# Batch 0's start refilled and batch 1's order changed in a fused cross-attention and GELU feed-forward kernel

## Chip, cores, metric

One core of a Trainium2 chip. The metric is the device time of one execution in microseconds (us), median over executions. Every execution used here also has a span (first to last instruction); in all of them the metric is the span plus 1.75 to 1.8 us, so the two can be compared by subtracting 1.77.

## The reference

For each of 8 batches and 8 heads, x (512 x 64) and a state (32 x 64) attend to one another: a softmax of x on state, and one of state on x. The 544 rows that come out per batch are then sent through a feed-forward layer.

```python
scores = scale * np.matmul(x, state.transpose(0, 1, 3, 2))
a = softmax(scores);  xread = np.matmul(a, state)
scores2 = scale * np.matmul(state, x.transpose(0, 1, 3, 2))
a2 = softmax(scores2); sread = np.matmul(a2, x)
x = concat([xread, sread])            # per batch (512+32) x (8*64)
h = x @ w_in                          # 512 -> 2048
g = 0.5 * h * (1.0 + erf(h / sqrt(2)))
return g @ w_out                      # 2048 -> 512
```

## The kernel before

The engines are PE (TensorE, products; PEld is its weight load), ACT (ScalarE), DVE (VectorE) and POOL (GpSimd). It never forms xread. It multiplies the state by w_in first (`P`, four quarters of 512 columns per batch), so that h is `P` times the transposed softmax `AT`. The order of instructions is written by hand; each engine takes its own in that order. `M(m)` is one tile of h (`hp` in the views) and its gelu (`g`), `U(u)` four products of an output tile (`op`), four tiles of g deep. Results of products land in PSUM, TensorE's result memory, and are copied from there by ACT or DVE. ACT does exps, gelus and some copies, DVE the rest.

```python
def keep_warm(n):                     # idle products, result unused
    ps = ps_o.tile([128, 512], FP32, name="warm_ps", tag="op")
    for _ in range(n):
        nc.tensor.matmul(ps[:, 0:128], lhsT=warm, rhs=warm, start=True, stop=True)

def norm(b, half):                    # row sums, reciprocal, product: all on DVE
    nc.vector.reduce_sum(out=cs, in_=e4, axis=AX.X)
    nc.vector.reciprocal(out=ics, in_=cs)
    nc.vector.tensor_tensor(out=..., in0=e4, in1=..., op=ALU.mult)

def pmat(b, fs, act=()):              # P = state x w_in, two halves t = 0, 1
    ...                               # 8 products into two PSUM tiles
    for t in range(2):
        if t in act: nc.scalar.copy(out=dst, in_=ps[t])
        else:        nc.vector.tensor_copy(out=dst, in_=ps[t])

begin(0)
keep_warm(30)
...                                   # batch 0: scores, softmax, transposes
M(0, 1, 2, 3)
U(0, 1)
pmat(0, (1,), act=(1,))
U(2)
M(4)
U(3)
state_prep(1, B)                      # state transposes of batches 1 to 7
M(5)
begin(1)
xtr(1, (0, 1))                        # x of batch 1 transposed
xtr(1, (2, 3))
sread(0)
M(6, 7)
scores(1, 0)
scores(1, 1)
srt(0)
U(4, 5)
pmat(0, (2,))                         # third quarter of P, BEFORE norm
rearr_ones(1)
norm(1, 0)
norm(1, 1)
U(6, 7)
M(8, 9)                               # first use of the third quarter
...
```

The softmax here doesn't subtract the row's maximum and nothing guards it: scores larger than these inputs give would overflow.

## Time and profile before

| | before |
|---|---|
| median of 4 | 219.09 us (218.79 to 219.24) |
| the execution whose profile is quoted in the prediction | 220.56 us, span 218.8 |
| TensorE busy | 213.5 us, 98% |

The profile's execution is 1.4 us longer than the median beside it. That gap turns out to matter. The lines on which the argument rests are in the prediction.

### The profile page before, as it was taken

What the parts mean: (1) busy time and instruction counts of PE and PEld (TensorE: products, weight loads), DVE (VectorE), ACT (ScalarE), POOL (GpSimd) and SP (SyncE); (2) the same over time, 40 slices, a digit from 0 to 9 for tenths busy, and PEclk for the clock granted to TensorE, in tenths of its full rate; (3) what the DMA queues carried; (4) which work ended last, traced back from release to release, by engine and by line L of the source; (5) the groups of instructions that cost most, each with busy time, mean ns of one, the idle gap of its engine ahead of it and who ended that gap; (6) DMA issues with size and microseconds to landing.
All of it is one profiled execution on the core that took longest, in us unless ns stands there. A gap on an engine that the chain in (4) does not pass through costs nothing.

```text
span 218.8 us, 3962 instructions
## 1 busy us (share of the span) xinstructions
PE 213.5 (98%) x1650; PEld 102.0 (47%) x1650; DVE 84.3 (39%) x165; ACT 121.9 (56%) x216; POOL 42.4 (19%) x56
## 2 busy tenths in 40 slices
PE   7999999999999999999999999999999999999993
PEld 6644534344444445444544444444444465565442
DVE  4722593626219230942176025902381204200151
ACT  3663765579494537953774479355944463564000
POOL 7662106700133011600170016000000000000000
PEclk9999999999999999999999999999999999999998
DMA  6999999960665818282725445370042002200035
GB/s 184 183 188 204 206 202 128 217 158 0 59 89 189 116 34 99 101 199 39 96 97 155 87 52 137 116 129 0 29 171 44 3 0 99 99 0 0 12 85 194
DMA packets 38708, 22.98 MB, mean 105 GB/s; under 512 B 21921, under 2 KB 34465, under 8 KB 38689
## 3 DMA queue, kind: packets, MB, share of 16 engines
q0 software_dynamic: 13648, 8.23, 27.2%
q1 hardware_dynamic: 24352, 14.09, 25.5%
q10 hardware_dynamic: 688, 0.39, 0.6%
q8 instruction: 13, 0.21, 0.4%
q14 instruction: 7, 0.05, 0.1%
HBM read 17.30 MB, written 8.91 MB: 120 GB/s over the span
## 4 chain that ended last, share of the span: by engine, by line
PE 97%; DVE 1%; ACT 1%; issue 0%
PE op L444 50%; PE hp L395 26%; PE p_ps L356 4%; PE hps L457 3%; PE ops L469 3%; PE warm_ps L127 2%; PE opl L422 2%; PE pt L263 2%; PE sr L319 1%; PE xT_ps L206 1%; PE pc L225 1%; ACT g L402 1%; PE p_ps L378 0%; PE aT_ps L299 0%; DVE xT L211 0%; PE st_ps L136 0%
## 5 line engine op out<-in xcount | busy, mean ns | idle before, releaser
L444 PE MATMUL op<-w_out_bf,g 128*128 128x512 bf16 x496 | 118.7, 379 | 0.1
L402 ACT ACTIVATE g<-hp 128x512 bf16<-128x512 f32 x128 | 67.9, 599 | 47.0 <-PE hp L395 46.9
L444 PEld LDWEIGHTS <-g 128*128 128x128 bf16 x496 | 47.0, 98 | 59.7 <-issue 6.6
L395 PE MATMUL hp<-AT,P 128*128 128x512 bf16 x256 | 66.1, 387 | 0.1
L395 PEld LDWEIGHTS <-P 128*128 128x128 bf16 x256 | 23.7, 99 | 27.4 <-issue 2.1
L408 DVE COPY osb<-op 128x512 f32<-128x512 f32 x31 | 20.9, 687 | 33.8 <-PE op L444 33.8
L370 DVE CAST P<-p_ps 128x512 bf16<-128x512 f32 x32 | 20.9, 686 | 31.3 <-PE p_ps L356 31.2
L368 ACT CAST P<-p_ps 128x512 bf16<-128x512 f32 x30 | 16.4, 588 | 23.1 <-PE p_ps L356 19.8
L170 POOL COPY x<-xb 128x1024 bf16<-128x1024 bf16 x12 | 12.1, 1041 | 31.1 <-DMA xb<-in_x_dram 26.1
L286 DVE TENSOR_TENSOR a<-e,ics 128x512 bf16<-128x512 bf16 x14 | 12.5, 892 | 0.5
L181 POOL COPY xo<-xb 128x1024 bf16<-128x1024 bf16 x12 | 12.2, 1050 | 0.0
L615 POOL COPY hold<-P 128x1 bf16<-128x1 bf16 x4 | 0.8, 190 | 53.8 <-DVE P L370 53.8
L283 DVE TENSOR_REDUCE cs<-e 128x16 f32<-128x512 bf16 x14 | 9.5, 676 | 2.5 <-ACT e L270 2.5
L356 PE MATMUL p_ps<-w_in_bf,sbd 64*32 64x512 bf16 x248 | 10.4, 382 | 0.0
L329 DVE RECIPROCAL inv<-sr 128x2 f32<-128x2 f32 x8 | 1.3, 168 | 22.8 <-PE sr L319 22.8
L270 ACT ACT_TABLE_LOAD x7 | 9.0, 1283 | 2.0 <-issue 1.3
L402 ACT ACT_TABLE_LOAD x7 | 9.0, 1283 | 0.1
L433 ACT COPY osb<-opl 128x128 f32<-128x128 f32 x1 | 0.3, 266 | 15.2 <-PE opl L422 15.2
L408 DVE COPY osb<-ops 128x512 f32<-128x512 f32 x2 | 1.4, 692 | 18.2 <-PE ops L469 18.2
L457 PE MATMUL hps<-XSR,w_in_bf 128*128 128x256 bf16 x64 | 8.3, 272 | 0.0
L270 ACT ACTIVATE e<-pt 128x512 bf16<-128x512 f32 x14 | 7.6, 594 | 0.1
L457 PEld LDWEIGHTS <-w_in_bf 128*128 128x128 bf16 x64 | 6.3, 98 | 2.4
(66 smaller groups left out, 112.5 us busy)
## 6 DMA issues: line engine op xcount, KB each, us to landing
out_dram<-osb SPq DMA_DIRECT2D x31, 256.0 KB, 2.3
xb<-in_x_dram POOLq DMA_DIRECT2D x7, 512.0 KB, 5.8
w_in_bf<-in_moe_w_in_dram POOLq DMA_DIRECT2D x8, 256.0 KB, 10.4
w_out_bf<-in_moe_w_out_dram POOLq DMA_DIRECT2D x4, 512.0 KB, 12.8
x0f<-in_x_dram SPq DMA_DIRECT2D x2, 256.0 KB, 3.4
out_dram<-osb SPq DMA_DIRECT2D x8, 64.0 KB, 1.7
x0f<-in_x_dram ACTq DMA_DIRECT2D x1, 256.0 KB, 4.2
st_bf<-in_state_dram POOLq DMA_DIRECT2D x1, 224.0 KB, 10.3
```

The source lines that it names most:

```text
L170: nc.gpsimd.tensor_copy(out=A.x4[:, :, :, 64 * t:64 * t + 64].rearrange("p j c d -> p c j d"), in_=src[:, t],)
L181: eng.tensor_copy(out=A.xo[:, :, c0:, 2 + 64 * t:66 + 64 * t].rearrange("p j c d -> p c j d"), in_=src[:, t, c0:],)
L270: nc.scalar.activation(out=A.e[:, :, 64 * half:64 * half + 64], in_=pt.rearrange("p j t c n -> p (j t) (c n)"), func=AF.Exp, scale=scale,)
L286: nc.vector.tensor_tensor(out=A.a[:, :, hs].rearrange("p g (c n) -> p g c n", n=NS), in0=e4, in1=ics[:, :, :].to_broadcast((128, G, 2, NS) ...
L356: nc.tensor.matmul(ps[t][32 * c:32 * c + 32, :], lhsT=sbd[64 * t:64 * t + 64, b, c, 32 * t:32 * t + 32], rhs=w_in_bf[64 * t:64 * t + 64, c ...
L368: nc.scalar.copy(out=dst, in_=ps[t])
L370: nc.vector.tensor_copy(out=dst, in_=ps[t])
L395: nc.tensor.matmul(hp, lhsT=Ps[b][:, t, m * 128:(m + 1) * 128], rhs=atts[b].AT[:, :, t, :], start=(t == 0), stop=(t == 1),)
L402: nc.scalar.activation(out=gs[b][:, m, :], in_=hp, func=AF.Gelu)
L408: nc.vector.tensor_copy(out=osb, in_=ps)
L444: nc.tensor.matmul(ps, lhsT=gs[b][:, m, j * 128:(j + 1) * 128], rhs=w_out_bf[:, m, :], start=(m == 0), stop=(m == MC - 1),)
L457: nc.tensor.matmul(hp, lhsT=w_in_bf[:, c, m * 128:(m + 1) * 128], rhs=XSR[:, c, :], start=(c == 0), stop=(c == HC - 1),)
```

## The change

Its intent: keep TensorE busy from the start so that its clock rises early, shorten batch 0's chain, and reorder loads and products to suit an earlier start. The diff is cut: unchanged lines between those shown are left out.

```diff
+    load_st(1, 2)            # states of batch 1 only, ahead of x of batch 1
-    (states of batches 1 to 7 in one load here)
         for f in range(2, FC):
             load_w_in(f); load_w_out(f)
+        load_st(2, B)
         load_x(2)
-        if b == 0 and cs[0] == 3:          # which xT copy of batch 0 ACT takes
+        if b == 0 and cs[0] == 2:
-                nc.scalar.copy(out=A.AT[:, :, t, :], in_=ps)
+                nc.vector.tensor_copy(out=A.AT[:, 0:2, t, :], in_=ps[:, 0:2, :])
+                nc.scalar.copy(out=A.AT[:, 2:4, t, :], in_=ps[:, 2:4, :])
-    keep_warm(30)
+    keep_warm(32)
     xtr(0, (0,))
+    keep_warm(6)
     xtr(0, (2,))
+    keep_warm(3)
-    sums0(2)
-    sums0(3)
+    sums0(2, 3)              # one instruction
     load_rest()
+    nc.scalar.activation(out=gate, in_=gate, func=AF.Gelu)   # moved up
+    keep_warm(2)
     p0 = pmat00(0)
...
     M(0, 1, 2, 3)
-    U(0, 1)
+    U(0, 1, 2)
     pmat(0, (1,), act=(1,))
-    U(2)
-    M(4)
     U(3)
-    state_prep(1, B)
-    M(5)
+    M(4, 5)
+    state_prep(1, 2)         # 2 to 7 later, after U(12)
+    M(6)
     begin(1)
...
-    M(6, 7)
+    M(7)
     scores(1, 0)
     scores(1, 1)
     srt(0)
     U(4, 5)
-    pmat(0, (2,))
     rearr_ones(1)
     norm(1, 0)
     norm(1, 1)
-    U(6, 7)
+    U(6)
+    pmat(0, (2,), act=(1,))
+    U(7)
     M(8, 9)
```

More of the change, by code (lines that the diff above doesn't have):

```diff
@@ L104, in load_x, with load_st @@
         xbs[b] = xb
+    def load_st(b0, b1):
+        nc.gpsimd.dma_start(
+            out=st_bf[:, b0:b1, :, :].rearrange("q b t d -> q (b t) d"),
+            in_=st_rows[:, b0:b1, :, :].rearrange("q b t d -> q (b t) d"),
+        )
     load_w_in(0)
@@ L108 @@
     load_w_in(1)
-    nc.gpsimd.dma_start(
-        out=st_bf[:, 1:B, :, :].rearrange("q b t d -> q (b t) d"),
-        in_=st_rows[:, 1:B, :, :].rearrange("q b t d -> q (b t) d"),
-    )
+    load_st(1, 2)
     def load_rest():
@@ L233, in scores0, with sums0 @@
         )
-    def sums0(c):
+    def sums0(*cs):
         A = atts[0]
-        if c % 2 == 0:
+        if cs[0] % 2 == 0:
             A.sums = att.tile([128, SJ * 2, 2], FP32, name="cs", tag="cs")
+        c0, n = cs[0], len(cs)
         nc.vector.reduce_sum(
-            out=A.sums[:, :, c % 2], in_=A.e[:, :, NS * c:NS * c + NS], axis=AX.X
+            out=A.sums[:, :, c0 % 2:c0 % 2 + n],
+            in_=A.e[:, :, NS * c0:NS * (c0 + n)].rearrange("p g (c n) -> p g c n", n=NS),
+            axis=AX.X,
         )
@@ L508 @@
     scores0(3)
-    sums0(2)
-    sums0(3)
+    sums0(2, 3)
     norm0(1)
     load_rest()
+    nc.scalar.activation(out=gate, in_=gate, func=AF.Gelu)
+    keep_warm(2)
     p0 = pmat00(0)
     nc.scalar.copy(out=Ps[0][:, 0, 0:512], in_=p0)
-    nc.scalar.activation(out=gate, in_=gate, func=AF.Gelu)
     keep_warm(10)
@@ L564 @@
     U(12)
+    state_prep(2, B)
     M(16)
```

## The prediction

> **What bounds the kernel now.** I read the page first (busy time and the chain that ended last), then the chain in order of time, then the timeline of the first 40 us.
>
> ```profile
> PE 213.5 (98%) x1650; PEld 102.0 (47%) x1650; DVE 84.3 (39%) x165; ACT 121.9 (56%) x216; POOL 42.4 (19%) x56
> PE 97%; DVE 1%; ACT 1%; issue 0%
> ```
>
> TensorE is busy 98% of the span and makes 97% of the chain that ended last. A change that leaves TensorE's real work alone, as this one does, can gain only where TensorE waits, runs idle products, or runs slowly. The list of waits has no TensorE wait worth naming after about 31 us; all of it lies at the start. The timeline there:
>
> ```profile
> 0.99 3.38 PE L127 MATMUL warm_ps<-warm 128*128 128x128 bf16 x30 [0.99 <-DVE warm L75]
> 5.71 0.39 PE L225 MATMUL pc<-sbd,xT 128*128 128x64 bf16 x4 [0.58 <-DVE xT L211]
> 8.54 0.39 ACT L228 ACTIVATE e<-pc 128x256 bf16<-128x256 f32 x1
> 9.55 0.42 DVE L239 TENSOR_REDUCE cs<-e 128x8 f32<-128x256 bf16 x1 [0.16 <-ACT e L228]
> 10.29 0.69 DVE L250 TENSOR_TENSOR a<-e,ics 128x512 bf16<-128x512 bf16 x1
> 11.48 1.06 PE L299 MATMUL aT_ps<-ident,a 128*128 128x128 bf16 x8
> 12.58 0.59 ACT L301 COPY AT<-aT_ps 128x512 bf16<-128x512 bf16 x1 [0.79 <-PE aT_ps L299]
> 12.63 3.71 PE L395 MATMUL hp<-AT,P 128*128 128x512 bf16 x8
> 16.16 2.13 PE L444 MATMUL op<-w_out_bf,g 128*128 128x512 bf16 x8
> 17.03 0.76 PEld L444 LDWEIGHTS <-g 128*128 128x128 bf16 x5 [0.53 <-ACT g L402]
> ...
> 43.27 2.32 PE L395 MATMUL hp<-AT,P 128*128 128x512 bf16 x10
> ```
>
> The columns are start, duration, engine, line. The line of most use is the eight hp products at 12.63: they take 3.71 us, while ten of the same at 43.27 take 2.32. With the last one's own 0.6 and 0.38 us taken off, the step from one to the next is (3.71-0.62)/7 = 0.44 us against (2.32-0.38)/9 = 0.216. TensorE runs at **half rate** until about 16.2 us. The thirty idle products (3.38 us, 0.107 each) and the transposes run at that half rate too; in the individual starts every 128-column product before 16.2 steps by 0.107, and the same after it by 0.056. The row PEclk of the page shows 9 in these slices and hides this: the trace's clock record has its first entry only at 16.2 us. So the idle products of the kernel before do not do their job: there are holes (0.25 us before the state transpose at 4.42, 0.58 before 5.71, 0.3 before 7.05, some 0.1 each at every change of tile), and the first stretch of over 3.4 us without a hole is the one from 12.63 on.
>
> **What the Trainium skill says.** (1) "TensorE: Matmul & The Clock Gate", Part 1, The HAM clock gate: the array starts at half clock, and goes to full after one busy window of about 3.4 us; the window runs free, so the moment varies by run. This trace agrees: half steps, and the change 3.57 us after the start of the first unbroken stretch. How large a hole still counts as busy the page does not say; here about 19% of holes in the 3.4 us before 12.8 was too much. (2) The same page, Part 4, PE-mode transpose: transposes don't count as busy in the same way. If so here, the transposes of batch 0 are holes too; no view of before settles it. (3) "ScalarE: Activation LUTs", What ACT_TABLE_LOAD costs: about 1283 ns; the trace has 1.28 us at 10.29. (4) "DMA: Bandwidth & Descriptors", Why small descriptors are slow: short pieces carry a fixed overhead. In the trace the 224 KB of states take from 14.64 to 16.12, 1.48 us, of which 1.27 (6/7) is for batches 2 to 7.
>
> **The change part by part.**
>
> Idle products: 30 to 32 adds 2x0.107 = 0.21 us, ending at 4.38 instead of 4.17, just before the state transpose that waits for ACT until 4.37, so it costs nothing and closes the 0.25 us hole. Six new ones (0.64) run from 4.92 to 5.56 in the hole before 5.71: free. Three (0.32) fill 6.75 to 7.07, where TensorE waits for DVE until 7.05: free within 0.03. Two more lie in front of the first P product. So TensorE is unbroken from 1.0 to about 7.3 but for some 0.15 us: 6.3 us, nearly two windows. I expect full clock at **about 4.6 to 6.0 us** instead of 16.2.
>
> Copies of batch 0: the third xT copy goes from DVE (0.42) to ACT (0.59), the fourth from ACT to DVE. The last two row sums (2 x 0.42) become one instruction of the 128x512 form, 0.68 in the groups. At half clock this alone moves little: the single sum must wait for the last exp, so 9.3+0.68 = 10.0 where now 9.55+0.42 = 9.97. At full clock the whole chain shortens: second xT ready at 6.80, scores and the two middle exps by 8.07, fourth xT 8.00, last exp 8.32 to 8.70, DVE sum to 9.42, reciprocal 0.25 to 9.69, product 0.69 to **10.40** (before 10.98).
>
> Transposes of a: before, TensorE reaches them only at 11.48, after ten idle products at half rate and the second P product at 10.75. At full rate these are over by 10.2 (its weights land at 9.62), so they start at 10.44; four take 0.45, DVE copies 0.43 to 11.31, the second half is copied by ACT (about 0.38, as the 128x256 copies) and DVE together to about 11.6. First hp product at 11.36 (before 12.63), second at 11.63 (before 13.22).
>
> hp, gelu, first output products: ACT then sets the pace. Four gelus in a row take 2.06 us (timeline at 59.32). First hp done at 12.0, so the fourth g at 14.1 and the fourth product of the first output tile at 14.15. Before, it waited for ACT till 17.04. That is **2.9 us earlier**. The table load and the gate's gelu move ahead of the P copy, which then ends at 10.8, still before 11.36: free.
>
> Transfers: w_in's second quarter (landed 14.64) and w_out's first (12.41) are in time for TensorE at 16.4 and 12.2. With 2.9 us gained x of batch 1 (landed 18.90) would be wanted at 18.9 and w_out's second quarter (21.88) at about 21.7, so both would just bind; moving the states of 2 to 7 behind the weights brings each at least 1.27 us forward. The later quarters have over 2 us in hand. x of batch 2 has the same bytes ahead of it (34.58), and its scores come at 47.6 while its xT landed at 42.05: 5.5 us in hand. The extra seven state transposes only move (0.39 us in all).
>
> Order of products: U(2) before the P products and M(6) earlier leave less work beside the batch 1 chain of xT copies (2 x 0.645), scores, softmax of the state read (0.16+0.29) and its transpose: I count 0.2 to 0.3 us of new waits near 20 us. The gelu wait at 31 us (about 0.6 lost on the output tile) stays, as the table load sits there still.
>
> Sum: -2.9 + 0.3 = **-2.6 us**, from 219.2 to **216.6**; after 31 us TensorE is full, so the gain is kept to the end.
>
> **The rivals.**
>
> A, the clock does not come early: transposes or the 0.1 us holes break the window. For: 1.7 of 4.9 us between 4.4 and 9.3 is transposes or tile changes. Against: the first 32 products and six more are nearly a whole window by themselves, and the reordering of loads and outputs makes sense only for an earlier start. Then only the split AT copy helps (second hp 0.2 us sooner): **218.7 to 219.1**.
>
> B, the timed runs of before are already faster at the start than the profiled one. The window is free-running, and a change one window earlier (12.8) would have ended the gelus near 16.1, 0.9 us sooner. Against: three timed runs lie within 0.25 us, where a random moment would spread more. Then the gain is 1.6 to 1.8: **217.4 to 217.6**.
>
> C, a transfer takes the place: x of batch 1 or the weights land late. Against: the landings above. It would return 0.5 to 1 us: **217.2 to 217.6**. D, the early clock is lost again because fewer products fill the stretch from 8 to 10.4; it would cost up to the hp part, and give about **217.7**.
>
> **Range and chances.** Early clock, about two in three, gives 216.6 (217.5 with B, C or D); otherwise 218.9. I put the point at **217.1 us**, between the main case and its discounts, with **216.1 to 218.9** to hold 8 in 10. Two per cent is 4.4 us, more than all half-rate and idle time at the start that I can find (before 17 us), so faster by over 2% is 0.03, within 2% 0.95, slower 0.02.
>
> **What would show it.** Right: idle products stepping at 0.056 instead of 0.107 before 9 us, eight hp products stepping at about 0.216 and starting near 11.4, the fourth output product near 14.2, DVE's product of batch 0 ending at 10.4, x of batch 1 landed by 17.6, no DMA wait of TensorE. Wrong: hp products still stepping at 0.43 (A); TensorE idle with a DMA as releaser between 16 and 30 us (C); or a kernel before whose other runs differ from its profile (B).

## The result

| | before | after |
|---|---|---|
| median of 4 | 219.09 us (218.79 to 219.24) | 220.67 us (220.51 to 221.59) |
| ratio | | 1.0083, 95% interval 1.0053 to 1.0112 |

Ratios are the mean of one kernel's fast runs over that of the other's of the same rounds, so not quite the ratio of the medians. The change is 0.8% slower; 1% faster was predicted.

The page of after, in the two lines that answer to those of before: TensorE does the same work and 13 idle products more in less busy time, and is no longer nearly all of the chain.

```profile
PE 210.0 (96%) x1663; PEld 100.2 (46%) x1663; DVE 83.8 (38%) x166; ACT 121.8 (56%) x217; POOL 43.3 (20%) x57
PE 89%; DMA 3%; DVE 2%; ACT 2%; POOL 1%; issue 1%; POOLq 0%; DVEq 0%
```

The timeline of after at the start (start, duration, engine, line, operation; in brackets the idle time before it and what ended it):

```profile
0.99 3.27 PE L132 MATMUL warm_ps<-warm 128*128 128x128 bf16 x32 [0.99 <-DVE warm L75]
5.80 0.29 PE L230 MATMUL pc<-sbd,xT 128*128 128x64 bf16 x4 [0.45 <-DVE xT L216]
8.32 0.38 ACT L233 ACTIVATE e<-pc 128x256 bf16<-128x256 f32 x1 [0.21 <-PE pc L230]
8.74 0.69 DVE L245 TENSOR_REDUCE cs<-e 128x16 f32<-128x512 bf16 x1 [0.19 <-ACT e L233]
9.75 0.69 DVE L258 TENSOR_TENSOR a<-e,ics 128x512 bf16<-128x512 bf16 x1
10.63 0.61 PE L307 MATMUL aT_ps<-ident,a 128*128 128x128 bf16 x8
11.71 0.37 ACT L310 COPY AT<-aT_ps 128x256 bf16<-128x256 bf16 x1 [1.01 <-DVE AT L309]
12.13 1.67 PE L404 MATMUL hp<-AT,P 128*128 128x512 bf16 x7 [0.23 <-ACT AT L310]
14.66 1.63 PEld L453 LDWEIGHTS <-g 128*128 128x128 bf16 x9 [0.39 <-ACT g L411]
```

Seven hp products take 1.67 us where eight took 3.71: full clock. The trace's clock record rises at 3.78 us. So the first half of the prediction held. The loss is later, in the timeline of after between 22 and 28 us:

```profile
23.94 0.69 DVE L291 TENSOR_REDUCE cs<-e 128x16 f32<-128x512 bf16 x1 [0.97 <-ACT e L278]
24.57 0.41 PE L365 MATMUL p_ps<-w_in_bf,sbd 64*32 64x512 bf16 x8
24.66 0.25 DVE L293 RECIPROCAL ics<-cs 128x16 f32<-128x16 f32 x1
24.95 0.69 DVE L294 TENSOR_TENSOR a<-e,ics 128x512 bf16<-128x512 bf16 x1
25.07 0.59 ACT L377 CAST P<-p_ps 128x512 bf16<-128x512 f32 x1 [0.67 <-PE p_ps L365]
25.56 0.68 DVE L291 TENSOR_REDUCE cs<-e 128x16 f32<-128x512 bf16 x1
26.34 0.25 DVE L293 RECIPROCAL ics<-cs 128x16 f32<-128x16 f32 x1
26.63 0.69 DVE L294 TENSOR_TENSOR a<-e,ics 128x512 bf16<-128x512 bf16 x1
27.24 0.68 DVE L379 CAST P<-p_ps 128x512 bf16<-128x512 f32 x1
27.98 1.04 PE L404 MATMUL hp<-AT,P 128*128 128x512 bf16 x4 [2.03 <-DVE P L379]
```

TensorE finishes the third quarter of P just before 25. ACT copies its half at 25.07. DVE's half stands in program order behind both halves of batch 1's softmax (L291, L293, L294, twice), so it starts only at 27.24, and TensorE idles **2.03 us**. Before, the same copies were next on DVE as soon as the products ended (timeline of before):

```profile
26.97 1.29 DVE L370 CAST P<-p_ps 128x512 bf16<-128x512 f32 x2 [1.87 <-PE p_ps L356]
28.57 1.03 PE L395 MATMUL hp<-AT,P 128*128 128x512 bf16 x4
```

Starts of the same events on TensorE, us (the clock's rise from the trace's clock record), from the timelines of four profiles (the second and fourth are experiments described below):

| event | before, quoted profile | before, second profile | after | idle products and loads only |
|---|---|---|---|---|
| clock rises | 16.20 | 13.20 | 3.78 | 6.12 |
| first hp | 12.63 | 12.69 | 11.53 | 11.45 |
| fourth output product | 17.04 | 16.03 | 14.66 | 14.36 |
| third quarter of P | 26.49 | 25.27 | 24.57 | 23.25 |
| first hp from it | 28.57 | 27.34 | 27.98 | 25.32 |
| fourth quarter of P | 31.99 | 30.76 | 31.64 | 28.74 |
| span | 218.8 | 217.5 | 218.7 | 215.8 |

After is ahead by 2.38 us of the quoted profile at the fourth output product, and by 1.37 of the second profile of before. It is ahead of the second by only 0.70 at the third quarter of P (having done one output group more by then), and 0.64 *behind* at the first hp that needs it.

### The profile page after: what moved, and what is told of

It is laid out like the page before. It is cut to its first block, busy times and chain, and to the rows that moved or that the text cites. A ratio compares the mean times of both kernels' runs of the same rounds, so it can differ in the third digit from the quotient of the medians.

```text
span 218.7 us, 3991 instructions
## 1 busy us (share of the span) xinstructions
PE 210.0 (96%) x1663; PEld 100.2 (46%) x1663; DVE 83.8 (38%) x166; ACT 121.8 (56%) x217; POOL 43.3 (20%) x57
## 4 chain that ended last, share of the span: by engine, by line
PE 89%; DMA 3%; DVE 2%; ACT 2%; POOL 1%; issue 1%; POOLq 0%; DVEq 0%
PE op L453 48%; PE hp L404 25%; PE p_ps L365 4%; PE hps L466 3%; PE ops L478 3%; DMA w_in_bf<-in_moe_w_in_dram 3%; PE opl L431 2%; PE sr L328 1%; PE pt L271 1%; ACT g L411 1%; DVE a L294 1%; DVE cs L291 1%; ACT L278 1%; PE xT_ps L211 0%; POOL xb L77 0%
## 5 line engine op out<-in xcount | busy, mean ns | idle before, releaser
L404 PE MATMUL hp<-AT,P 128*128 128x512 bf16 x256 | 64.5, 379 | 2.7 <-DVE P L379 2.0
L379 DVE CAST P<-p_ps 128x512 bf16<-128x512 f32 x31 | 20.3, 686 | 30.9 <-PE p_ps L365 30.7
L377 ACT CAST P<-p_ps 128x512 bf16<-128x512 f32 x31 | 17.0, 588 | 24.4 <-PE p_ps L365 21.3
L294 DVE TENSOR_TENSOR a<-e,ics 128x512 bf16<-128x512 bf16 x14 | 12.0, 859 | 0.5
L291 DVE TENSOR_REDUCE cs<-e 128x16 f32<-128x512 bf16 x14 | 9.5, 675 | 3.4 <-ACT e L278 3.4
```

The source lines that it names most:

```text
L294: nc.vector.tensor_tensor(out=A.a[:, :, hs].rearrange("p g (c n) -> p g c n", n=NS), in0=e4, in1=ics[:, :, :].to_broadcast((128, G, 2, NS) ...
L404: nc.tensor.matmul(hp, lhsT=Ps[b][:, t, m * 128:(m + 1) * 128], rhs=atts[b].AT[:, :, t, :], start=(t == 0), stop=(t == 1),)
```

## The experiments

Theory O: the P copy behind batch 1's softmax costs what the start gains, and more. Theory B: before's clock moment varies, and the quoted profile was a late one. Rivals are in each expectation. All runs were correct, and the record lists every one as fast; where I say slow below, I mean a longer run with a lower mean granted clock. The kernels were run in three jobs (experiments 1 to 4, 5 to 8, 9 to 12); those of one job share the chip and the runs of before.

**1. Before once more.** No edit.

> The kernel before once more, to see its clock. Theory B (the moment of full clock varies by run, and the profiled run of before at 16.2 us was one of the late ones): this profile may show the step from 0.107 to 0.056 us per 128-column product at another moment, near 12.8, 9.4 or earlier, and then a span near 217.3 instead of 218.8. Rival (the moment is fixed at 16.2 us and the profiled run is longer for another reason): step at 16.2 again, span 218.8. Ratio to before 1.000.

Median 218.67 us of 14, ratio 0.9993. The clock rose at 13.20 us this time, span 217.5. Theory B holds for the two executions that were profiled; for the others only the times are known, as the mean granted clock does not show the moment (0.997 in the quoted execution, 1.000 here). Over three chips, before's 124 runs for comparison spread from 217.99 to 220.79, and only six, 220.49 and above, are about as long as the profile I worked from (220.56). The timeline of this profile has the eight hp products at

```profile
12.69 2.26 PE L395 MATMUL hp<-AT,P 128*128 128x512 bf16 x8
```

in 2.26 us instead of 3.71.

**2. P first.** After, with the third quarter of P ahead of the softmax:

```diff
     U(4, 5)
+    pmat(0, (2,), act=(1,))
     rearr_ones(1)
     norm(1, 0)
     norm(1, 1)
     U(6)
-    pmat(0, (2,), act=(1,))
     U(7)
```

> The kernel after with the third P products moved back ahead of batch 1's row sums and products in program order, nothing else. Theory O (the P copy that TensorE waits for stands behind batch 1's softmax on DVE, 2.0 us of idle TensorE at 26 us): that wait goes, span 216.7, ratio to before 0.990 to 0.995. Rival (the loss is from the loads or idle products, and the idle at 26 us only moves): TensorE idle over 1 us elsewhere before 32 us, ratio 1.005 to 1.009.

Median 218.25 us of 23, ratio 0.9972 (0.9960 to 0.9984), against 1.0083 and 1.0099 for after, which was not run in this job: **one moved line is worth about 2.4 us** (2.4 to 2.8 by these ratios). The ratio is a little short of what I expected (0.990 to 0.995), since before's average is faster than its quoted profile. The DVE timeline of this run shows the copy ahead of the softmax:

```profile
25.48 0.69 DVE L379 CAST P<-p_ps 128x512 bf16<-128x512 f32 x1 [1.87 <-PE p_ps L365]
26.09 0.75 DVE L186 COPY xo<-xb 128x1024 bf16<-128x1024 bf16 x2
26.76 0.68 DVE L291 TENSOR_REDUCE cs<-e 128x16 f32<-128x512 bf16 x1
```

Its profiled execution (219.45) was the one slow one of the 23: the clock record shows full clock from 4.03 to 10.86, half from 10.86 to 14.27 (one stretch of 3.413 us), then full.

**3. The old order.** After, with the order of products of before (the state transposes still split), the third quarter of P copied wholly by DVE.

```diff
-    U(0, 1, 2)  ...  M(4, 5) ... M(6) ... M(7) ... norm ... U(6), pmat(0, (2,), act=(1,)), U(7)
+    U(0, 1)     ...  M(4)    ... M(5) ... M(6, 7) ... U(4, 5), pmat(0, (2,)), norm ..., U(6, 7)
```

> The kernel after with the whole order of products of before (only the state transposes stay split in two). Theory O: like the run with P first, 216.5 to 217.0 of span, ratio 0.990 to 0.995. If x of batch 1 or the third quarter of w_in comes too late for this order, TensorE idles with a DMA as releaser, and the ratio is 0.995 to 1.0.

Median 218.00 us of 12, ratio 0.9954 (0.9934 to 0.9973), span 216.3 (expected 216.5 to 217.0). No wait for a DMA from 10 us on. Everything of the change but the order of products is thus a gain of about 0.9 us (by the medians of this job).

**4. Idle products only.** Before, with 32, 6, 3 and 2 idle products as in after.

```diff
-    keep_warm(30)
+    keep_warm(32)
     xtr(0, (0,))
+    keep_warm(6)
     xtr(0, (2,))
+    keep_warm(3)
     load_rest()
+    keep_warm(2)
```

> The kernel before with the idle products of after (32, 6, 3 and 2) and nothing else. If the clock alone is worth what I predicted: full clock before 6 us in the profile, span 217 or less, ratio to before 0.990 to 0.997. If before is mostly at full clock by 12.8 us already (theory B): ratio 0.997 to 1.000.

Median 218.83 us of 14, ratio 0.9995 (0.9981 to 1.0010), though full clock came at 3.79 in its profile. This is theory B's number; but B is not the whole reason. At the second quarter of P this run is 1.23 us ahead of the second profile of before (15.76 against 16.99), at the transposes of batch 1's x 0.76, and 0.55 from the third quarter's hp on. The timelines of this run show where:

```profile
18.67 0.59 PE L395 MATMUL hp<-AT,P 128*128 128x512 bf16 x2
19.67 1.08 PE L206 MATMUL xT_ps<-ident,xb 128*64 128x128 bf16 x32 [0.41 <-DMA xb<-in_x_dram]
```

x of batch 1 landed at 19.63. A second transfer takes more of the lead: the last part of w_in's third quarter landed at 24.67, and the products that need it took 0.86 us instead of 0.41:

```profile
24.27 0.86 PE L356 MATMUL p_ps<-w_in_bf,sbd 64*32 64x512 bf16 x8
24.72 0.11 PEld L356 LDWEIGHTS <-sbd 64*32 64x32 bf16 x7 [0.36 <-DMA w_in_bf<-in_moe_w_in_dram]
```

The early clock alone only brings TensorE to these two transfers sooner.

**5. After once more.** No edit.

> The kernel after once more, on the same chip as its variants and with more runs of before. Theory O (2.0 us of idle TensorE behind the P copy on DVE, against a gain at the start of about 1 us over the average run of before, whose clock moment varies): ratio to before 1.005 to 1.009, spread narrower than before's except for runs that lose the clock again. If the first result was the chip's or the day's: 0.997 to 1.003.

Median 221.13 us of 6, ratio 1.0099 (1.0069 to 1.0129). The six fall in two groups: 220.64 to 220.68 with a mean granted clock of 0.998, and 221.58 to 221.69 with 0.990 to 0.992. One 3.413 us stretch at half clock would lower the mean by 0.5 x 3.413 / 219 = 0.008.

**6. Both P copies on ACT.** After, order untouched:

```diff
-    pmat(0, (2,), act=(1,))
+    pmat(0, (2,), act=(0, 1))
```

> The kernel after, its order of products untouched, but both P copies of the third quarter on ACT, so none stands behind batch 1's softmax on DVE. Theory O: the wait for DVE's P copy at 26 us goes; ACT is free at 25.1, so both copies end by 26.3, but the gelu table load behind them ends 0.6 later than in after: gain of 1.3 to 2.0 us over after, ratio to before 0.997 to 1.001. Rival (TensorE runs into the gelus or the softmax chain anyway): gain under 0.5 us, ratio 1.003 to 1.008.

Median 218.73 us of 22, ratio 0.9986 (0.9974 to 0.9999). Against experiment 5, in the same job, the medians differ by 2.4 us; against the faster of its two groups (220.65) it is 1.9. So the loss comes back by another route than in experiment 2: no order was changed, only the engine. That shows theory O. The timeline shows TensorE at 25.72 where after had 27.98:

```profile
24.97 1.07 ACT L377 CAST P<-p_ps 128x512 bf16<-128x512 f32 x2 [0.64 <-PE p_ps L365]
25.72 1.21 PE L404 MATMUL hp<-AT,P 128*128 128x512 bf16 x4
```

None of the 22 runs (218.64 to 219.21) is in a slow group.

**7. Loads only.** Before, with the states of 2 to 7 behind the weights and their transposes after U(12).

```diff
-    (states 1 to 7)
+    load_st(1, 2)
+        load_st(2, B)        # ahead of load_x(2)
-    state_prep(1, B)
+    state_prep(1, 2)
     U(12)
+    state_prep(2, B)
```

> The kernel before with the loads of after only (states of batches 2 to 7 behind the weights, their transposes after the thirteenth output product group). With the clock moment of before (10 to 13.5 us mostly) TensorE reaches x of batch 1 no earlier than it lands, so the loads free at most a few tenths: ratio 0.997 to 1.000. Rival (x of batch 1 bounds the kernel before too): 0.995 or less.

Median 218.17 us of 22, ratio 0.9979 (0.9958 to 1.0001), from 217.41 to 220.31. The profiled execution (217.47) had, with before's own 30 idle products, full clock at 3.88: so this start can be early too. By their times I take it that an early run of before is held at 218 by the transfers of experiment 4, that early runs without these waits get to 217.4, and that late ones stay at 220.3; only one run of this kernel was profiled, so this is not shown. The expectation (few tenths) held on average, but not its reason.

**8. Idle products and loads.** Both edits together.

> Idle products and loads of after together, the rest as before. In the run with idle products alone TensorE was 1.2 us ahead at the second P products (15.8 us) but only 0.55 from 27 us on, since x of batch 1 landed at 19.6. Theory (the two parts need one another): ratio 0.995 to 0.9975, near the 0.9954 of the old-order run, so that the copies and row sums are worth 0.0 to 0.4 us. Rival (the copies and sums make the gain): 0.998 to 1.000.

Median 217.77 us of 10 (217.62 to 218.20), ratio 0.9944 (0.9920 to 0.9968). The two parts give 0.05% and 0.2% alone, and 0.56% together. The three intervals are about as wide as what the sum lacks (0.3%), so the times alone hardly show that the parts need one another; the traces do. The second takes away the waits that the first runs into, and the first brings the early clock: full clock came between 3.78 and 6.28 in all ten profiles with after's idle products, but in only one of the four with before's 30 (3.88; the others 13.20, 13.48 and 16.20). The same lines as in experiment 4, without the wait:

```profile
18.13 0.60 PE L399 MATMUL hp<-AT,P 128*128 128x512 bf16 x2
18.65 1.08 PE L210 MATMUL xT_ps<-ident,xb 128*64 128x128 bf16 x32
```

**9. Order only.** Before, with after's order of products.

```diff
-    U(0, 1) ... pmat(0, (2,)), rearr_ones(1), norm(1, 0), norm(1, 1), U(6, 7)
+    U(0, 1, 2) ... rearr_ones(1), norm(1, 0), norm(1, 1), U(6), pmat(0, (2,), act=(1,)), U(7)
```

> The kernel before with the new order of products of after and nothing else. Theory O: the wait of TensorE for the P copy behind batch 1's softmax comes here too, as that chain hangs on the exps and not on the start: TensorE idle 1.0 us or more before the hp products of the third quarter with DVE's P copy as releaser, ratio to before 1.005 to 1.012. Rival (the order only costs with an early start): 0.998 to 1.003.

Median 221.62 us of 6, ratio 1.0103 (1.0067 to 1.0140). Its profile has the same wait, without the new start:

```profile
28.83 0.68 DVE L370 CAST P<-p_ps 128x512 bf16<-128x512 f32 x1
29.57 1.04 PE L395 MATMUL hp<-AT,P 128*128 128x512 bf16 x4 [1.75 <-DVE P L370]
```

**10. The second AT copy whole.** The old-order run, with that copy on ACT as before.

```diff
-                nc.vector.tensor_copy(out=A.AT[:, 0:2, t, :], in_=ps[:, 0:2, :])
-                nc.scalar.copy(out=A.AT[:, 2:4, t, :], in_=ps[:, 2:4, :])
+                nc.scalar.copy(out=A.AT[:, :, t, :], in_=ps)
```

> The old-order run, but the second half of the transposed a copied whole by ACT as in before, the sums, the swapped xT copies and the gate's place as in after. In after the ACT half of the split copy starts only when DVE's half has ended (11.71 against 11.69), though its data was there 0.4 us earlier. Theory: the second hp product comes 0.38 us after the first instead of 0.60, gain of 0.2 us over the old-order run, ratio 0.993 to 0.995. Rival (the split is harmless): as the old-order run, 0.995 to 0.9965.

Median 217.81 us of 15, ratio 0.9945 (0.9929 to 0.9961). In the profile the second hp product comes 0.38 us after the first (11.45 and 11.83), against 0.60 with the split (11.71 and 12.31). In the split, ACT's half begins when DVE's ends, though they touch different columns. The Trainium skill, "PSUM — Partial Sum Buffer", PSUM bank collisions raise a hardware error, says that two engines may not touch one bank and partition quadrant at once, so that software orders them; the halves here are read from one PSUM tile, and the trace of after shows them one after the other (11.71 for ACT after DVE's 11.39 + 0.28). In this run ACT's whole copy (11.19) reads another PSUM tile than DVE's copy (10.97 + 0.42) and overlaps it, though both write the one tile AT. The 0.2 us are plain in the trace; as the two runs were on different chips and the intervals overlap, the time does not resolve them.

**11. More idle products in after.**

```diff
-    keep_warm(2)
+    keep_warm(12)
     p0 = pmat00(0)
-    keep_warm(10)
+    keep_warm(16)
     p1 = pmat00(1)
```

> The kernel after with ten more idle products before the first P product and six more before the second, where TensorE waits for w_in. Half of the runs of after are 1 us longer (221.6 against 220.65), and in the run with P first the profile caught one that lost full clock from 10.86 to 14.27. Theory H (the slower half is such a loss, as TensorE is idle in between): the group at 221.6 goes, all runs 220.5 to 220.9, median 220.7. Rival (other cause): the two groups stay.

Median 221.21 us of 6, ratio 1.0105 (1.0069 to 1.0142). The two groups stay: three runs at 220.55 to 220.77, three at 221.64 to 221.80 (clock 0.991 to 0.992). Theory H, that holes at 8 to 10 us make the slow half of after's runs, fell. What is left: the 2.03 us wait at 26 us itself makes TensorE idle for 59% of a 3.413 us stretch that contains it. Slow runs are 7 of 16 in the kernels with this wait; such a stretch contains the whole wait in (3.41-2.03)/3.41 = 40% of its positions. After's variants without that wait lose the group but for one of 23 in experiment 2. Against it: mean clocks of 0.984 to 0.992 are also found in 13 of 160 runs of before and of experiment 7, which have no such wait; and the order-only run, with a wait of 1.75, has none among 6, its profile keeping full clock through a stretch that holds the whole wait. No profile caught a slow run of after, so the cause of its slow group stays open.

**12. Idle products and loads again**, beside experiment 10.

> Idle products and loads together once more, on the same chip as the run with the whole ACT copy, to tell what copies and sums are worth: against that run, equal within 0.001 if sums and swapped copies do nothing (theory), lower by 0.001 or more if they cost, higher if they gain. Ratio to before 0.9935 to 0.996.

Median 217.84 us of 14, ratio 0.9940 (0.9918 to 0.9961): the same as experiment 10 (0.9945). The new row sum, the swapped xT copies and the gate's earlier place are worth nothing that these runs resolve. This version, idle products and loads, beats both kernels: **0.6% faster than before**, and 1.4 to 1.6% faster than after by the ratios.

## Why the prediction was wrong

- **Early clock, 4.6 to 6.0 us: right, though the moment varies more.** 3.78 in after's profile, 3.8 to 6.3 in the profiles with the same idle products.
- **Batch 0's chain: right but for one link.** DVE's product ended at 10.44 (10.40 predicted), the first hp started at 11.53 (11.36). The second hp came at 12.13 instead of 11.63: the two halves of the AT copy were taken as parallel, and ran one after the other. The fourth output product came at 14.66 (14.15).
- **The step that failed** is "Order of products: ... I count 0.2 to 0.3 us of new waits near 20 us". I looked at the chain near 20 us and not at DVE's program order after it. Moving the third P products behind the softmax put one 0.68 us copy behind 3.3 us of row sums and products (23.94 to 27.24). Measured: 2.03 us of idle TensorE at 26 us, where 0.2 to 0.3 was counted. Experiments 2, 6 and 9 remove it twice and bring it in once, by about 2.4, 1.9 to 2.4 and about 2.4 us of run time. Every kernel with the order of after, but for the one with both copies on ACT, is slower than before.
- **The term of -2.9 was mis-sized as well.** Against the quoted profile it was 2.38; against the second profile of before, 1.37. Rival B was true, and I gave it too little: three runs within 0.25 us spoke against a random moment, but the quoted profile's own time, 220.56 beside a median of 219.18, spoke for it and was in hand. A sum worked out on a 218.8 us span was taken off a 219.2 us time that belongs to a span of 217.4.
- **Transfers: half right.** x of batch 1 landed at 18.37, not by 17.6, but TensorE reached it at 19.39 without a wait. Alone, without the loads, the earlier start does run into it (experiment 4), as the prediction said. It also runs into w_in's third quarter there, of which the prediction said "over 2 us in hand": in the quoted profile it landed at 23.99 for products that start at 26.49, which is 2.5 us before, and less than nothing after, a gain of 2.9. With the loads moved it landed at 23.55 in after, in time for 24.57. In after TensorE also waited 0.48 and 0.24 us for w_in near 9 to 10 us.
- **Sum for after against the second profile of before:** ahead 1.57 at the third quarter of P (0.70, and 0.87 for the output group done earlier), behind by 2.21 for the wait (counted from start to start; 2.03 of it idle), 0.24 between 28 and 32 us, and 0.33 after that, which is about what the state transposes take that only moved (0.34). That is 1.21 behind, and the spans differ by 218.7 - 217.5 = 1.2.

## What to carry to other kernels

Here DVE took its instructions in the order of the program (23.94 to 27.24 us in after), so moving products past a softmax also moved their copies behind it: for each moved group, list what stands in front of its copy out of PSUM on the copying engine. Before working from one profile, set its own time beside the median: a profile from the tail of the distribution makes the gain look larger than it is. Two edits that do little alone (0.05% and 0.2% here, for an earlier start and for the loads that would have held it) can give more together (0.6%), so test them in pairs.

## What the Trainium skill lacked or had wrong

- "TensorE: Matmul & The Clock Gate", the table of Why this matters for your kernels, asks for no idle gap of TensorE over some 3 us. In the P-first profile the longest gap before the loss was 1.01 us, and full clock was still lost for 3.413 us. By my count (each product from its start to its end less 0.165 us of drain, an estimate) TensorE was busy 42% of the 3.413 us before the loss. That is no border either: full clock was kept through stretches of 53% in after, 40% in the loads-only profile (3.88 to 7.29) and 41% in the order-only one (27.13 to 30.55).
- The same page, Part 1, doesn't say how busy a window must be to raise the clock. By the same count the clock rose after stretches of 0.82 to 0.98 (fourteen profiles), and did not after one of 0.84 in the quoted profile of before (16% of holes; the prediction put it at 19%). The two overlap, so these runs give no border.
- The same page, Part 1: the spread of the moment is given as 0.5 us, for sustained activity, and no figure for a start with holes. Here one kernel rose at 16.20 in one execution and 13.20 in another, and the loads-only run, with the same idle products as before, at 3.88; the run times of before spread by 2.8 us.
- The same page, Part 4, on transposes not counting as busy: no run here tests it. They do run faster at full clock: the eight transposes of a took 1.06 us at half clock in before, and 0.61 at full clock in after.
